# Linear attention with decay feeding a SiLU block: attention by pairs of chunks in 64x64 array tiles

## The chip, the cores and the metric

The kernel runs on one core of a Trainium2 chip. The metric is the device time of one execution in microseconds; the median of three runs is given. Engines are named as in the profile: PE is TensorE (matmul; PEld its weight loads), DVE is VectorE, ACT is ScalarE, POOL is GpSimd, SP is SyncE, which here only issues DMAs.

## What is computed

Two stages, with `q`, `k`, `v` of shape (4, 8, 768, 64) (batch, heads, positions, head dimension) and a decay `lam` per head:

```python
for b in range(nb):                       # blocks of 64 positions
    intra = (qb @ kb.T * Dmask) @ vb      # Dmask[i, j] = lam ** (i - j) for i >= j, else 0
    inter = (qb * lam_pow) @ kv_state     # lam_pow[i] = lam ** (i + 1)
    out[:, :, sl] = intra + inter
    kv_state = lam ** 64 * kv_state + (kb * rev_pow).T @ vb
x = out.transpose(0, 2, 1, 3).reshape(3072, 512)
h = x @ w_in                              # 512 -> 2048
y = (h * sigmoid(h)) @ w_out              # 2048 -> 512
```

All inputs and the output are float32. The kernel works in bf16 on TensorE with float32 sums. The result does not depend on the block length, so a kernel may choose its own chunks.

## The kernel before

**Units.** Attention is worked off in 24 units `u` of U = 128 positions (four batches of six). For each unit, k, q and v come as tiles with a position in each of 128 partitions and (head, dimension) along the row, so that a DMA piece is 64 floats, 256 B. For the first `EARLY` = 8 units all three come as float32 on SP's queue (`raw`, L313), k and q are cast by ACT or DVE into `kq` (L277, L279) and turned by TensorE with an identity (`tr`, L402), then copied to `kqT`. For later units k and q come on POOL's queue, cast on the way (L316), and are turned by a DMA transpose on SP's queue (L416); v still comes by SP. `vd` is v times a power of lam for its position (L284, called from L386).

**Attention of a unit** (heads in `NP` = 4 pairs `m`, a pair filling 128 partitions):
- scores `st_ps` (L427): 8 matmuls of a 64x128 array tile with 128 columns, the two heads of a pair in two row halves; masked by `tri_e` into `st` in two DVE operations
- the new state `d_ps` (L446): 8 matmuls of 128x64 with 64 columns, for all but the last unit of a batch
- from it and the running state `xf`: `y` (L458, add), `xe` (bf16, times lam to the power U) and the next `xf`
- the outputs `x_ps` (L481): 8 matmuls of 128x64 (`st` and `vd`) and, unless the unit is the first of its batch, 8 of 64x64 (`xe` and `kqT`, the term of the state), all summed in one bank
- `xt` (L498): `x_ps` times a power of lam for the query's position, in bf16. This is x, transposed, ready for the first product.

**The two products.** `product1` takes groups of one, two or four units (`groups`): `h_ps` (L518) has 128, 256 or 512 columns per matmul, 512 columns per PSUM bank; ACT applies SiLU (L532) into `g`. `product2` makes a unit's 128 rows of output in `o_ps` (L552), 16 matmuls of 512 columns (of 256, twice, for the first six units and the last), copied by ACT or DVE and stored on ACT's queue.

**Weights.** `w_in` (blocks i0 to i3) and `w_out` (o0 to o3) come on POOL's queue, cast to bf16 on the way. `sequence` (L340) sets the order of loads; POOL reads one element of a landed load (`gated`, L293) before it issues weights, so that the first units' loads get ahead of them.

**Order.** The program is a list of tasks with a key, a cost per engine and the tasks that it depends on. `Planner.order` runs them through a small model of engines, buffers and queues before anything is issued and fixes, once, the order of instructions on every engine. On the chip each engine goes through its list and stops at each instruction until its inputs are there; nothing is reordered. `POOLS` is the number of buffers of each kind; the eight PSUM banks are one pool, `att` allows at most five of them to attention, `one` four to `h_ps` and `two` two to `o_ps`.

Of the kernel before, what the change touches and what calls it, by code (L numbers as in the profile page):

```python
# [8 lines left out]
F32 = mybir.dt.float32  # L9
BF16 = mybir.dt.bfloat16  # L10
# [24 lines left out]
SMALL, CAST, LARGE, HALF, TURN = (256, 16.4, 18.5), (256, 14.0, 31.0), (2048, 92.0, 92.0), (1024, 58.0, 58.0), (1024, 46.0, 46.0)  # L35


class Planner:
# [5 lines left out]
    BEGIN = {"PE": 0.8, "ACT": 6.0, "DVE": 2.7, "POOL": 3.4, "SP": 0.8}  # L44
    FIRST, LAST, AHEAD = {"SP": 1.15, "ACT": 1.15, "POOL": 2.5}, 1.0, 0.75
# [13 lines left out]
    def order(self):  # L59
# [12 lines left out]
        queues = {e: [] for e in ("SP", "POOL", "ACT")}  # L72
        clock = [0.0]
# [49 lines left out]
        while len(out) < len(self.tasks):  # L123
# [9 lines left out]
            for e in free:  # L133
# [34 lines left out]
                free[e] = now + t.on[e]  # L168
                heapq.heappush(events, free[e])
# [20 lines left out]
def kernel(  # L190
# [13 lines left out]
    U = 128  # L204
    NB = S // U
    NU = B * NB
# [4 lines left out]
    EARLY = 8  # L211
# [6 lines left out]
    POOLS = dict(bank=8, raw=9, rv=4, kq=6, kqT=5, vd=4, st=3, xe=3, y=3, xf=3,  # L218
                 xt1=4, xt2=2, xt4=2, g=40, osb=3, osh=4, one=4, two=2, att=5)
# [3 lines left out]
    def tile_of(b, shape, dt, name):  # L223
        if b.tile is None:
            pool = ps if b.pool == "bank" else sb
            b.tile = pool.tile(shape, dt, tag=f"{b.pool}{b.slot}", name=name)
        return b.tile
# [15 lines left out]
    iota_p = const.tile([128, 1], mybir.dt.int32, name="iota_p")  # L243
    nc.gpsimd.iota(iota_p, pattern=[[0, 1]], base=0, channel_multiplier=1)
    row_i = const.tile([128, U], mybir.dt.int32, name="row_i")
    nc.gpsimd.iota(row_i, pattern=[[1, U]], base=-64, channel_multiplier=0)
    tri_e = const.tile([128, U], F32, name="tri_e")
    nc.gpsimd.memset(tri_e, 1.0)
    nc.gpsimd.affine_select(
        out=tri_e, in_=tri_e, compare_op=AL.is_ge, fill=0.0,  # L250
        base=0, pattern=[[1, U]], channel_multiplier=-1,
    )
    pose = const.tile([128, 1], F32, name="pose")
    nc.vector.tensor_scalar(pose, iota_p, -1.0, 64.0, op0=AL.mult, op1=AL.add)
    row = const.tile([128, U], F32, name="row")
    nc.vector.tensor_copy(row, row_i)
# [6 lines left out]
    lam_v = const.tile([128, H], F32, name="lam_v")  # L263
    lam_xe = const.tile([128, NP, U], F32, name="lam_xe")
    lam_be = const.tile([128, NP], F32, name="lam_be")
    nc.scalar.activation(lam_v, log_all, AF.Exp, scale=pose[:, 0:1])
# [20 lines left out]


    gate = const.tile([128, 8], F32, name="gate")
# [17 lines left out]
    def load_unit(key, u):  # L307
        b, blk = divmod(u, NB)
        src = [x[b, :, blk * U:blk * U + U, :].rearrange("h s d -> s h d") for x in (k, q, v)]
        kq, bufs, ts = Buf("kq"), [None] * 3, [None] * 3  # L310

        def plain(e, i):
            nc.sync.dma_start(out=tile_of(bufs[i], [128, H, 64], F32, "raw"), in_=src[i])  # L313

        def casting(e, i):
            nc.gpsimd.dma_start(out=tile_of(kq, [128, 2, H, 64], BF16, "kq")[:, i], in_=src[i])  # L316

        for i in range(3):
            if u < EARLY or i == 2:
                bufs[i] = Buf("raw" if u < EARLY else "rv")  # L320
                ts[i] = add((key, i), {"SP": 0.55}, lambda e, i=i: plain(e, i), bufs=[bufs[i]], nbytes=0.262, kind=SMALL,
                            late=0.3 if u < EARLY else LATE)
            else:
                ts[i] = pool_load((key, i), 0.92, lambda e, i=i: casting(e, i), [kq], 0.262, CAST, LATE)
        raw[u] = kq, bufs, ts
# [3 lines left out]
    def load_w(key, what, j):  # L329
        def go(e):  # L330
            if what == "i":
                cs = slice(512 * j, 512 * j + 512)
                nc.gpsimd.dma_start(out=w_in_bf[:, :, cs], in_=w_in_r[:, :, cs])
            else:
                ks, cs = slice(8 * (j % 2), 8 * (j % 2) + 8), slice(256 * (j // 2), 256 * (j // 2) + 256)
                nc.gpsimd.dma_start(out=w_out_bf[:, ks, cs], in_=w_out_r[:, ks, cs])

        wload[what, j] = [pool_load((key, 0), 0.8, go, [], 1.0486, LARGE if what == "i" else HALF, 1.0)]

    sequence = "u0 i0 i1 u1 i2 u2 i3 u3 u4 u5 u6 o0 o1 u7 o2 o3".split() + [f"u{u}" for u in range(EARLY, NU)]  # L340
    unit, last = None, None
    for n, x in enumerate(sequence):
        j = int(x[1:])
        if x[0] == "u":
            load_unit(n - 100, j)
            unit = j
        else:
            if last != unit and unit < EARLY:
                _, bufs, loads = raw[unit]
                gated((n - 100, -1), loads[0], unit, lambda buf=bufs[0]: buf.tile[:, 0, 0:1])  # L350
                last = unit
            load_w(n - 100, x[0], j)


    groups = [[0], [1], [2], [3], [4, 5], [6, 7], [8, 9], [10, 11]] + [list(range(4 * n, 4 * n + 4)) for n in range(3, NU // 4)]
    group_of = {u: (gi, i) for gi, us in enumerate(groups) for i, u in enumerate(us)}
    xt = [Buf(f"xt{len(us)}") for us in groups]
    xt_done = [[] for _ in groups]
    carry = {}

    chain = {}

    def after(stage, ts):

        ts = ts if isinstance(ts, list) else [ts]
        for t in ts:
            t.deps += chain.get(stage, [])
        chain[stage] = ts

    def Bank():  # L370
        return Buf("bank", Buf("att"))

    def attention(u):
        s = u - 4.0 if u < 4 else u - 5.5
        kq, bufs, (lk, lq, lv) = raw[u]
        kqT, vd, st = Buf("kqT"), Buf("vd"), Buf("st")
        gi, gp = group_of[u]

        def kq_of():
            return tile_of(kq, [128, 2, H, 64], BF16, "kq")  # L380

        def cast(e, i):
            copy(e, kq_of()[:, i], bufs[i].tile)

        def scale_v(e):
            mult(e, tile_of(vd, [128, H, 64], BF16, "vd"), bufs[2].tile,  # L386
                 lam_v[:, :, None].to_broadcast([128, H, 64]))

        if u < EARLY:
            ck = [add((s - 1.0, i), {"DVE": 0.43, "ACT": 0.63}, lambda e, i=i: cast(e, i), deps=[(lk, lq)[i]],  # L390
                      bufs=[bufs[i], kq]) for i in range(2)]
            after("k", ck)
        else:
            ck = [lk, lq]
        cv = add((s - 0.8, 0), {"DVE": 0.7}, scale_v, deps=[lv], bufs=[bufs[2], vd])

        after("v", cv)
        turned = []

        def turn(e, i, m):  # L400
            t = tile_of(banks[i], [128, NP, U], BF16, "tr")
            nc.tensor.transpose(t[:, m, :], kq_of()[:, i, 2 * m:2 * m + 2, :], ident)  # L402

        def t_of():
            return tile_of(kqT, [128, 2, NP, U], BF16, "kqT")

        if u < EARLY:
            banks = Bank(), Bank()
            for i in range(2):
                ts = [add((s - 0.7, i, m), {"PE": 0.056}, lambda e, i=i, m=m: turn(e, i, m), deps=[ck[i]],  # L410
                          bufs=[banks[i], kq]) for m in range(NP)]
                turned.append(add((s - 1.0, 2), {"DVE": 0.65, "ACT": 0.6},
                                  lambda e, i=i: copy(e, t_of()[:, i], banks[i].tile), deps=ts, bufs=[banks[i], kqT]))
        else:
            def dma_turn(e):
                nc.sync.dma_start_transpose(t_of().rearrange("p i m s -> p (i m) s"),  # L416
                                            kq_of().rearrange("p i h d -> p (i h d)"))

            turned.append(add((-150.0, u), {"SP": 1.4}, dma_turn, deps=ck, bufs=[kq, kqT], nbytes=0.393, kind=TURN,
                              late=2.0))  # L420

        st_ps = [Bank() for _ in range(2)]

        def score(e, m):
            for h, r in enumerate(halves):
                t = tile_of(st_ps[h], [128, NP, U], F32, "st_ps")
                nc.tensor.matmul(t[:, m, :], lhsT=t_of()[r, 0, m, :], rhs=t_of()[r, 1, m, :], start=True, stop=True)  # L427

        sc = [add((s - 0.55 + 0.02 * m, 0), {"PE": 0.062}, lambda e, m=m: score(e, m), deps=turned + chain.get("m", []), bufs=st_ps + [kqT])
              for m in range(NP)]  # L430
        mk = [add((s - 0.9, 0), {"DVE": 0.69},
                  lambda e, h=h: mult(e, tile_of(st, [128, 2, NP, U], BF16, "st")[:, h], st_ps[h].tile,
                                      tri_e[:, None, :].to_broadcast([128, NP, U])),
                  deps=sc, bufs=[st_ps[h], st]) for h in range(2)]

        after("s", sc)
        chain["m"] = mk
# [134 lines left out]

    for u in range(NU):
        attention(u)
# [37 lines left out]
```

## Time and profile before

| what | value |
|---|---|
| median of 3 runs | 233.63 us (233.47 to 233.82) |
| the profiled execution | 233.32 us |
| its span, first to last instruction | 231.6 us |
| granted TensorE clock, mean | 0.993 |
| h_ps, L518 | 700 matmuls in the trace, 115.9 us busy |
| o_ps, L552 | 482 matmuls, 105.4 us busy |
| SiLU on ACT, L532 | 96 of 598 ns |
| mask on DVE, st <- st_ps | 48 of 685 ns |
| evacuation xt <- x_ps on DVE | 24 of 688 ns |
| cast loads of k and q on POOL's queue | 32 of 128 KB written |
| transposes on SP's queue | 16 |
| DMA moved | 29.67 MB, 92544 of 102677 packets under 512 B |

Busy times of TensorE overlap, as matmuls are pipelined: what one costs in a stream is the distance from its start to the next start. The page shows the span in 40 slices of 5.8 us, with a digit for the busy share of each engine; a DMA share over 1.00 in the table by stages means that packets of several queues overlap on an engine.

### The profile page before, as it was taken

The page shows a single profiled execution, that of the slowest core. Times are in us where ns is not written, and L with a number is a line of the kernel's source. Part 1 is how long each engine was busy: PE and PEld are TensorE (multiplying, and loading weights), DVE is VectorE, ACT ScalarE, POOL GpSimd, SP SyncE. Part 2 cuts the span into 40 slices and gives each one's busy share as a digit, 9 for nine tenths or more (in the row PEclk, how much of TensorE's full clock was granted, in tenths as well). Part 3 has the DMA queues.
Part 4 walks back from the last instruction along what each step waited for, and adds up shares of the span by engine and source line. Part 5 has one row for each costly group of instructions (what it writes and reads, how often), then busy time and mean ns, then how long its engine had stood idle before and what let it go on. Part 6 is the DMA issues. An engine that isn't in the chain of part 4 may idle for free.

```text
span 231.6 us, 4583 instructions
## 1 busy us (share of the span) xinstructions
PE 212.2 (92%) x1950; PEld 134.5 (58%) x1968; DVE 89.4 (39%) x165; ACT 82.7 (36%) x149; POOL 41.3 (18%) x61
## 2 busy tenths in 40 slices
PE   0547889999999999999999999999999999999994
PEld 0336778878888884686754444444444444444453
DVE  1445285766130007555574663556542111110100
ACT  5431625684433221242521146522323333333221
POOL 3403014922240003350333341011100000000000
PEclk9999979999999999999999999999999999999999
DMA  5999999999999985999999999610101111001112
GB/s 120 203 196 232 217 211 216 167 185 182 159 174 197 152 228 67 195 120 147 167 146 195 193 157 172 123 48 0 48 3 42 48 48 45 14 31 48 73 63 91
DMA packets 102677, 29.67 MB, mean 128 GB/s; under 512 B 92544, under 2 KB 100480, under 8 KB 102656
## 3 DMA queue, kind: packets, MB, share of 16 engines
q0 software_dynamic: 39552, 8.39, 41.3%
q1 hardware_dynamic: 58496, 14.68, 37.8%
q10 hardware_dynamic: 4608, 6.30, 7.9%
q8 instruction: 15, 0.25, 0.4%
q14 instruction: 6, 0.05, 0.1%
HBM read 27.27 MB, written 6.29 MB: 145 GB/s over the span
## 4 chain that ended last, share of the span: by engine, by line
PE 87%; DMA 6%; SPq 2%; DVE 1%; ACT 1%; issue 1%
PE h_ps L518 38%; PE o_ps L552 36%; PE x_ps L481 7%; DMA raw<-in_v_dram 6%; PE d_ps L446 3%; PE st_ps L427 3%; SPq L313 2%; PE tr L402 1%; DVE xt L284 1%; ACT g L532 0%; DVE vd L284 0%; ACT kqT L277 0%; ACT kq L277 0%; DVE xe L284 0%; DVE kqT L279 0%
## 5 line engine op out<-in xcount | busy, mean ns | idle before, releaser
L518 PE MATMUL h_ps<-xt,w_in_bf 128*128 128x128 bf16 (+2 forms) x700 | 115.9, 290 | 1.1 <-DVE xt L284 0.6
L552 PE MATMUL o_ps<-w_out_bf,g 128*128 128x512 bf16 (+1 forms) x482 | 105.4, 330 | 0.7 <-issue 0.5
L532 ACT ACTIVATE g<-h_ps 128x512 bf16<-128x512 f32 x96 | 56.6, 598 | 95.9 <-PE h_ps L518 91.6
L518 PEld LDWEIGHTS <-w_in_bf 128*128 128x128 bf16 x704 | 60.4, 102 | 27.0 <-issue 1.1
L552 PEld LDWEIGHTS <-g 128*128 128x128 bf16 x496 | 47.5, 98 | 32.3
L284 DVE TENSOR_TENSOR st<-st_ps,tri_e 128x512 bf16<-128x512 f32 x48 | 30.9, 685 | 32.1 <-PE st_ps L427 32.1
L279 DVE COPY osb<-o_ps 128x512 f32<-128x512 f32 (+1 forms) x11 | 6.8, 619 | 54.7 <-PE o_ps L552 53.0
L316 POOL DMA_DIRECT2D kq<-in_k_dram x16 | 14.1, 883 | 61.8 <-PE x_ps L481 56.3
L277 ACT ACTIVATE osb<-o_ps 128x256 f32<-128x256 f32 (+1 forms) x20 | 9.6, 479 | 36.0 <-PE o_ps L552 31.0
L284 DVE TENSOR_TENSOR xt<-x_ps,lam_xe 128x512 bf16<-128x512 f32 x24 | 16.5, 688 | 6.3 <-PE x_ps L481 5.9
L402 PE MATMUL tr<-ident,kq 128*128 128x128 bf16 x64 | 7.3, 242 | 11.4 <-POOL gate L293 5.7
L284 DVE TENSOR_TENSOR vd<-raw,lam_v 128x512 bf16<-128x512 f32 x24 | 16.2, 683 | 2.9 <-DMA raw<-in_v_dram 2.9
L316 POOL DMA_DIRECT2D kq<-in_q_dram x16 | 14.2, 890 | 7.3 <-DMA w_out_bf<-in_moe_w_out_dram 6.3
L458 DVE TENSOR_TENSOR y<-d_ps,xf 128x256 f32<-128x256 f32 x16 | 6.8, 425 | 18.5 <-PE d_ps L446 18.5
L277 ACT ACTIVATE kqT<-tr 128x512 bf16<-128x512 bf16 x14 | 8.4, 597 | 11.0 <-PE tr L402 10.9
L284 POOL TENSOR_TENSOR xf<-y,lam_be 128x256 f32<-128x256 f32 x6 | 3.7, 611 | 47.9 <-DVE y L458 47.9
L402 PEld LDWEIGHTS <-kq 128*128 128x128 bf16 x64 | 4.5, 106 | 12.6 <-DVE kq L279 9.3
L427 PE MATMUL st_ps<-kqT 64*128 64x128 bf16 x192 | 10.2, 229 | 1.6 <-ACT kqT L277 0.9
L481 PE MATMUL x_ps<-kqT,xe 64*64 64x128 bf16 x160 | 11.1, 231 | 0.0
L481 PE MATMUL x_ps<-st,vd 128*64 128x128 bf16 x192 | 11.0, 235 | 0.0
L427 PEld LDWEIGHTS <-kqT 64*128 64x128 bf16 x192 | 6.0, 98 | 8.4 <-issue 7.8
L446 PE MATMUL d_ps<-vd,kq 128*64 128x64 bf16 x160 | 9.0, 209 | 1.5 <-DVE vd L284 1.5
(32 smaller groups left out, 55.3 us busy)
## 6 DMA issues: line engine op xcount, KB each, us to landing
raw<-in_v_dram SPq DMA_DIRECT2D x24, 256.0 KB, 6.3
out_dram<-osb ACTq DMA_DIRECT2D x17, 256.0 KB, 2.1
raw<-in_k_dram SPq DMA_DIRECT2D x8, 256.0 KB, 4.9
raw<-in_q_dram SPq DMA_DIRECT2D x8, 256.0 KB, 6.2
w_in_bf<-in_moe_w_in_dram POOLq DMA_DIRECT2D x4, 512.0 KB, 8.0
w_out_bf<-in_moe_w_out_dram POOLq DMA_DIRECT2D x4, 512.0 KB, 13.8
kq<-in_k_dram POOLq DMA_DIRECT2D x16, 128.0 KB, 5.2
kq<-in_q_dram POOLq DMA_DIRECT2D x16, 128.0 KB, 6.5
```

What stands on the lines that cost most here:

```text
L277: nc.scalar.activation(o, i, AF.Copy)
L279: nc.vector.tensor_copy(o, i)
L284: (nc.vector if e == "DVE" else nc.gpsimd).tensor_tensor(o, a, b, op=AL.mult)
L316: nc.gpsimd.dma_start(out=tile_of(kq, [128, 2, H, 64], BF16, "kq")[:, i], in_=src[i])
L402: nc.tensor.transpose(t[:, m, :], kq_of()[:, i, 2 * m:2 * m + 2, :], ident)
L427: nc.tensor.matmul(t[:, m, :], lhsT=t_of()[r, 0, m, :], rhs=t_of()[r, 1, m, :], start=True, stop=True)
L446: nc.tensor.matmul(t[r, m, :], lhsT=kq_of()[:, 0, 2 * m + h, :], rhs=vd.tile[:, 2 * m + h, :], start=True, stop=True)
L458: nc.vector.tensor_tensor(tile_of(src, [128, NP, 64], F32, "y"), d_ps.tile, xf[0].tile, op=AL.add)
L481: nc.tensor.matmul(t[r, m, :], lhsT=lhsT(h, r), rhs=rhs(h, r), start=first, stop=True, skip_group_check=True)
L518: nc.tensor.matmul(t[:, j, :], lhsT=w_in_bf[:, ko, 128 * m:128 * m + 128], rhs=xt[gi].tile[:, ko, :], start=(ko == 0), stop=(ko == KI - 1))
L532: nc.scalar.activation(tile_of(g, [128, per, n], BF16, "g"), bank.tile, AF.Silu)
L552: nc.tensor.matmul(t, lhsT=g.tile[:, j, 128 * gp:128 * gp + 128], rhs=w_out_bf[:, ko, cs], start=(ko == 0), stop=(ko == KO - 1))
```

## The change

Attention goes by 12 pairs of chunks: a pair is 256 positions, a partition holds two neighbouring positions (r = 0, 1) and the partition halves are the two chunks `c` of 128 positions. A row of a load is then two positions, 512 B (later k and q, which are cast on the way, still come in rows of 256 B, one DMA for each r).

- **Tiles.** Scores, outputs and states are all matmuls of 64x64 tiles, with the loops so that four neighbours lie in the four places of the array. The term of the states is a plain 128x128 matmul: `xe` is now a block-diagonal 128x128 matrix for each pair of heads (`xe_all`, zeroed once, then only the two diagonal blocks are written, each by its own DVE operation).
- **Two bursts.** The eight heads go in two halves `g`. After the mask of half i: the states' term and the outputs of half i, the states of the next pair (if i is a pair's second half), the scores of half i+1.
- **PSUM.** `st2` (scores, two banks) and `xd` (outputs and new states, two banks) have one tile each; four single banks stay for `h_ps` (`one`: three), `o_ps` (`two`) and the transposes.
- **Start.** `EARLY` = 5 pairs (ten units) come as float32 and are turned by TensorE; pair 0 comes in two halves of heads (`FINE`). The first group of `product1` has 256 columns and starts on the first two of its four slices when half the heads are done. The first weights wait for v of pair 0's second half (`g0v`), i2 and i3 for k of pair 1, o2 and o3 for k of pair 3.
- **w_out** comes in four blocks of 4x128 whole rows; `product2` uses 512 columns for all but the last unit.
- **Planner.** A switch between tiled and plain matmuls is given 0.095 us.

```diff
-    EARLY = 8
+    EARLY = 5
+    FINE = (0,)
...
-    POOLS = dict(bank=8, raw=9, rv=4, kq=6, kqT=5, vd=4, st=3, xe=3, y=3, xf=3,
-                 xt1=4, xt2=2, xt4=2, g=40, osb=3, osh=4, one=4, two=2, att=5)
+    POOLS = dict(bank=4, st2=1, xd=1, raw=6, rawh=6, rv=3, kq=4, kqT=3, vd=3, st=2, xe=4, y=2, xf=3,
+                 xt2=4, xt4=2, g=40, osb=3, osh=4, one=3, two=2)
...
+    xe_all = const.tile([128, POOLS["xe"], NP, 128], BF16, name="xe_all")
+    nc.vector.memset(xe_all, 0.0)
...
+        def plain(e, i, g, ms):
+            nc.sync.dma_start(out=tile_of(bufs[i, g], [128, 2 * len(ms), 128], F32, "raw"),
+                              in_=src[i][heads(ms)].rearrange("h (p r) d -> p h (r d)", r=2))
+        def casting(e, i, r):
+            nc.gpsimd.dma_start(out=tile_of(kq, [128, 2, 2, H, 64], BF16, "kq")[:, i, r],
+                                in_=src[i].rearrange("h (p r) d -> r p h d", r=2)[r])
...
-    sequence = "u0 i0 i1 u1 i2 u2 i3 u3 u4 u5 u6 o0 o1 u7 o2 o3".split() + [f"u{u}" for u in range(EARLY, NU)]
+    sequence = "u0 g0v i0 i1 u1 g1k i2 i3 u2 u3 o0 o1 g3k o2 o3 u4".split() 
+    sequence += [f"u{n}" for n in range(NU // 2) if f"u{n}" not in sequence]
...
-    groups = [[0], [1], [2], [3], [4, 5], [6, 7], [8, 9], [10, 11]] + [list(range(4 * n, 4 * n + 4)) for n in range(3, NU // 4)]
+    groups = [[0, 1], [2, 3], [4, 5], [6, 7], [8, 9], [10, 11]] + [list(range(4 * n, 4 * n + 4)) for n in range(3, NU // 4)]
...
+        def states(e, ms):
+            t = duo_tile(at)
+            for m in ms:
+                for r in range(2):
+                    for c, p in enumerate(halves[:1] if final else halves):
+                        for h, d in enumerate(halves):
+                            nc.tensor.matmul(t[d, c, 256 + 64 * m:320 + 64 * m], lhsT=kq_of()[p, 0, r, 2 * m + h, :],
+                                             rhs=vd.tile[p, 2 * m + h, r, :], start=first_in(box, c, h), stop=True,
+                                             skip_group_check=True)
...
+                for m in range(2):
+                    for r in range(2):
+                        for c in halves:
+                            for h, d in enumerate(halves):
+                                nc.tensor.matmul(t[c, h, m, r, :], lhsT=t_of()[d, 0, r, 2 * g + m, c],
+                                                 rhs=t_of()[d, 1, :, 2 * g + m, c], start=(m == 0 and r == 0), stop=True,
+                                                 skip_group_check=True)
...
+            def inter(e, i=i, g=g, used=used, box=box_x):
+                t = duo_tile(i)
+                for m in range(2):
+                    for c, x in used:
+                        nc.tensor.matmul(t[:, c, U * m:U * m + U], lhsT=xe_of(x[0])[:, 2 * g + m, :],
+                                         rhs=t_of()[:, 1, :, 2 * g + m, halves[c]],
+                                         start=first_in(box, c, 0) | first_in(box, c, 1), stop=True, skip_group_check=True)
```

## The prediction

> **What bounds the kernel now.** I read the page's busy table and slices first, then the stages, then the chain and single bursts on TensorE.
>
> ```profile
> PE 212.2 (92%) x1950; PEld 134.5 (58%) x1968; DVE 89.4 (39%) x165; ACT 82.7 (36%) x149; POOL 41.3 (18%) x61
> ...
> PE   0547889999999999999999999999999999999994
> ...
> DMA  5999999999999985999999999610101111001112
> ...
> q1 hardware_dynamic: 58496, 14.68, 37.8%
> q10 hardware_dynamic: 4608, 6.30, 7.9%
> ```
>
> From slice 7 on (about 35 us) TensorE is full, although DMA is full too until 75 us. So there are two places to gain: TensorE's work after 32 us, and the holes before it. By stage (us, TensorE busy, loads, DVE, ACT, POOL, clock, DMA):
>
> ```profile
> 0.00:16.70 16.70, 5.07 (x56) 3.34 (x56) 5.33 (x12) 7.49 (x16) 4.36 (x15) 1.00 1.00 172
> 16.70:21.00 4.30, 2.80 (x37) 2.31 (x34) 1.94 (x4) 0.80 (x2) 0.00 (x0) 1.00 1.22 230
> 21.00:32.00 11.00, 9.66 (x136) 8.55 (x136) 5.57 (x13) 5.08 (x9) 2.48 (x4) 0.95 1.19 219
> 32.00:60.00 28.00, 27.43 (x412) 23.35 (x409) 17.21 (x33) 16.43 (x30) 10.71 (x14) 0.96 1.26 187
> 60.00:175.00 115.00, 114.00 (x1051) 71.10 (x1064) 54.53 (x99) 36.58 (x65) 23.74 (x28) 1.00 1.09 135
> ```
>
> Over 98% busy from 32 us, and DVE and ACT under two thirds there: in that part only fewer or denser TensorE instructions shorten the kernel.
>
> One unit of attention (128 positions) costs TensorE two bursts between the big products (start, length, what):
>
> ```profile
> 160.63 0.38 PE L518 MATMUL h_ps<-xt,w_in_bf 128*128 128x512 bf16 x1
> 160.94 0.40 PE L427 MATMUL st_ps<-kqT 64*128 64x128 bf16 x8
> 161.27 0.39 PE L552 MATMUL o_ps<-w_out_bf,g 128*128 128x512 bf16 x1
> ...
> 162.79 0.38 PE L518 MATMUL h_ps<-xt,w_in_bf 128*128 128x512 bf16 x1
> 163.10 0.28 PE L446 MATMUL d_ps<-vd,kq 128*64 128x64 bf16 x6
> 163.32 0.24 PE L481 MATMUL x_ps<-kqT,xe 64*64 64x128 bf16 x2
> 163.49 0.22 PE L446 MATMUL d_ps<-vd,kq 128*64 128x64 bf16 x2
> 163.64 0.35 PE L481 MATMUL x_ps<-kqT,xe 64*64 64x128 bf16 x6
> 163.93 0.41 PE L481 MATMUL x_ps<-st,vd 128*64 128x128 bf16 x8
> 164.27 0.39 PE L552 MATMUL o_ps<-w_out_bf,g 128*128 128x512 bf16 x1
> ```
>
> Big products with 512 columns start 0.216 us apart (162.36, 162.58, 162.79 in the timeline). So the first burst adds 161.27-160.63-0.216 = 0.42 us and the second 164.27-162.79-0.216 = 1.26. The reader should see the price of a change of array shape: st_ps starts 0.31 after the last h_ps instead of 0.216, so 0.095 going in; its last pair starts at 161.12 and the next product at 161.27, 0.15 instead of 0.056, so 0.09 coming out. The second burst changes shape four times inside.
>
> **TensorE, steady part.** Removed: 24 x 0.42 for scores, 16 full second bursts at 1.26, four first units of a batch without the states' term (read the same way at 112.35 us: 0.57) and four last without a new state (174.63: 0.78): 10.2+20.2+2.3+3.1 = 35.8 us.
>
> Added, per pair of chunks (256 positions): 32 score and 32 output matmuls of 64x64 tiles with 128 columns, 32 state matmuls with 64 columns, and 8 plain matmuls for the states' term. In the trace two tiles in different places start 2 to 4 ns apart and the next two 56 ns later (128 columns), or 26 to 32 ns later (64 columns, d_ps). Four tiles at once are not shown, nor 64x64 tiles in four places; two sharing rows (x_ps from vd, d_ps), two sharing columns with different banks (st_ps) and two on the diagonal (xe) are. Bounds: four at a time, 4.5/4 = 1.13 us per pair (64 x 0.056 + 32 x 0.029 = 4.5), and one at a time, 4.5. I take four, since each pairing of places occurs, and the weight loads of d_ps follow each other within some 12 ns on average. Plain: 8 x 0.056 = 0.45, the spacing of h_ps with 128 columns, which these have too. Switches: two bursts, each in and out, 4 x 0.095 = 0.38. Pair: 1.13+0.45+0.38 = 1.96. Twelve make 23.5; the four first pairs of a batch lack half of the plain ones (-0.9), the four last half of the states (-0.5); I add 0.8 for four extra spells in the first pairs, where data come in halves. Sum 22.9, a gain of **12.9 us**.
>
> Transposes on TensorE go from 64 to 80 (five pairs instead of eight units): +0.9. The four 128-column groups of h_ps become 256 wide: by 0.056 against 0.108 per product -0.3 at the most.
>
> **Other engines in that part.** The mask stays at 1.37 us per unit (2 x 0.685), now as one operation of 1024. The state xe is written by two half-partition operations each: 0.43 x 2 more per pair, 10 us on DVE over the kernel, and two more units are cast and copied by DVE and ACT instead of arriving cast (2 x (2 x 0.6 + 2 x 0.6) = 5 us). DVE at 39% and ACT at 36% hide this while each burst has some 8 us to the next (two bursts in 2 x (6.9+1) us); the chain states, y, xe, xf, y, xe of about 3 us must fit there too. Without that cover it would be 15 us. SP issues 25 loads and 7 transposes instead of 40 and 16, POOL 28 casts instead of 32: lighter queues, priced at nothing, as TensorE waited for neither after 32 us. The whole-row stores of the first six units (6 instead of 12 on ACT) and w_out by rows of 1024 B instead of 512 end in the backlog of h_ps work and are priced at nothing too. The memset of xe_all stands on DVE ahead of pose and row; four times a bf16 512-column result at 0.69 bounds it at 2.8 us, so done by 3.6, and ACT's first Ln waits for lam until 4.01: hidden (else vd, at 7.69, moves by as much).
>
> **Waits added.** Scores and outputs have one PSUM tile each. Scores already wait for the mask before; outputs now wait also for the evacuation before (0.69) and for y reading the states in the same tile (two of 0.43), some 2 us against 8 between bursts. The second outputs of a pair wait for the next pair's transpose and vd: behind them on TensorE stand all big products in its order, so a late transpose would stop TensorE by as much as it is late. Its loads are issued two or three pairs (16 us each) ahead and a transpose lands in 5.3 us for half the size: nothing.
>
> **The start.** On full speed the work done by 32 us is 96 h_ps x 0.056, 36 transposes x 0.056 and three and a half units of attention (4.8): 12.2 us, so 19.8 us are lost there. What decides is when loads land. First, rows of 512 B. q1 (nearly all 256-B packets): 37.8% of 16 x 231.6 us over 58496 packets is 23.9 ns each; q10 (mean 1367 B) 63.5 ns. The straight line gives 33 ns for 512 B against 2 x 23.9, so 0.69 of the time. Bounds: no gain, and half. The casts of k and q, and vd, of unit 0 begin as their loads land, at 5.20, 6.41, 7.69: 1.2 us per 256 KB, which becomes 0.85.
>
> Second, a moved gate: POOL's first weights wait for the first unit's k now (gate at 5.23, issue 5.61) and would wait for v of the second half of pair 0, the sixth piece: 5.2 + 5 x 0.85 = 9.5. Behind the gate on POOL stand all weights. The four w_in blocks land now 6.7, 9.1, 10.2 and 6.9 us after issue (12.3, 15.7, 19.1, 29.0). From 9.9 on the first lands at 16.6, the others 3.7 apart (20, 24, 28), as the second gate, k of pair 1, has passed by then (pair 1 streams from 8 to 13 us while POOL waits). So the first h_ps comes at 16.6, as now (16.76). But then two pairs are ready instead of one unit: each block feeds 2 x 16 x 0.108 = 3.5 us of h_ps. Work: 13.8 h_ps, 4 attention, 1.8 transposes; until about 20 us it runs at half speed (h_ps 16.76: 16 in 1.89 us). I get its end at 34 to 35 us, so 15 us lost: a gain of **5.0 us**. Ends: 0 (plan and arrivals disagree, as for v at 19.4 now, where TensorE stood 1.5 us), and 9 (19.6 us of work done by 31). I take the middle for the order of each engine's work is fixed and slips are likely.
>
> [...]
>
> **Sum.** Span 231.6 - 12.9 + 0.9 - 0.3 - 5.0 = 214.3. The profiled execution took 233.32, 1.7 more than its span; the median is 233.63, 0.3 more again. Forecast **216.3 us**, by itself 211 to 220.
>
> **Rivals.**
> A, the start gains nothing, or bursts don't merge (outputs and scores apart: 2 more spells a pair, 12 x 0.38 = 4.6): 221. For it: the gate is 4.3 us later and plans slip. Against: two pairs feed each block. Chance 0.17.
>
> B, only two tiles at a time: per pair 2.25+0.83 = 3.08, 13.4 us more: 230. For it: four were never seen. Chance 0.08.
>
> C, slower, by PSUM: eight banks shared become four for h_ps, o_ps and transposes, since scores and outputs hold two each for good. With three h_ps banks of 0.86 us each ACT must return one in 2.6 us; silu is 0.6, but casts and copies of pairs are 1024 wide (2 x 0.63) and stand ahead of it in ACT's queue. It decides the sign from 17 us, 0.18 for each of 96 banks; at 0.2 each, 19 us: 235. Against: ACT waited 91.6 us for h_ps, TensorE none for ACT there. Chance 0.06.
>
> D, slower: column tiles load weights one after another, so that no two tiles overlap: 96 x 0.029 to 0.056, 4.5+0.83 = 5.33 per pair, 40 us more than forecast: 257. Break-even is at 1.75 tiles at a time. d_ps starts six 64-column loads within 60 ns, which speaks against: 0.03. [...]
>
> **How the numbers follow.** Forecast 0.66, A 0.17, B 0.08, C 0.06, D 0.03. The range 210 to 225 holds forecast and A. About 0.2% can be told from no change; near zero falls next to nothing: faster 0.90, same 0.01, slower 0.09.
>
> **What would show it.** Spells of tiled matmuls two per pair, each about 0.9 to 1.1 us between big products; four tiles starting within 15 ns; the first h_ps near 16.6 with few gaps after; TensorE busy over 98% from 35 us. Wrong if TensorE waits for ACT g or xt in the middle, if tiles come 28 ns apart, or if the first w_in lands after 18.

## The result, and the profile after

The changed kernel takes 274.5 us (273.19 to 278.7, 4 runs) against 233.55 for the kernel before: a ratio of 1.1746 (95% interval 1.1672 to 1.182). Some runs show a lower granted clock and take longer; the ratios leave them out, here the one of 278.7 us. Forecast were 216.3 us, with 210 to 225 as the range. The profiled execution took 273.79 us, with a span of 271.9.

The page of the changed kernel: busy times, and the slices of TensorE, of its granted clock and of DMA (40 slices of 6.8 us).

```profile
PE 210.8 (78%) x2198; PEld 125.8 (46%) x2224; DVE 100.9 (37%) x162; ACT 83.1 (31%) x138; POOL 33.7 (12%) x51
...
PE   1669999989970069839199999999999999999400
...
PEclk9999999999995559977869999999999999999955
DMA  5999999999945999999998383011001111111110
```

TensorE has no more to do than before (210.8 us busy against 212.2); the 40 us are holes, around slice 13, around slices 18 and 20, and at the end, and stretches at half clock. The stages of the changed kernel (columns as before: stage, length, then TensorE, its loads, DVE, ACT, POOL, clock, DMA, GB/s):

```profile
21.00:32.00 11.00, 11.00 (x134) 8.98 (x133) 5.75 (x11) 6.63 (x10) 0.00 (x0) 1.00 1.19 216
...
78.00:98.00 20.00, 2.25 (x57) 1.55 (x55) 0.69 (x1) 0.00 (x0) 1.75 (x2) 0.60 1.09 77
98.00:127.00 29.00, 22.42 (x236) 13.23 (x233) 13.60 (x20) 4.56 (x8) 7.00 (x8) 0.80 1.97 127
127.00:260.00 133.00, 120.68 (x1041) 63.02 (x1052) 41.34 (x64) 38.05 (x65) 3.51 (x4) 0.97 0.39 52
260.00:272.00 12.00, 0.00 (x0) 0.00 (x0) 0.00 (x0) 0.00 (x0) 0.00 (x0) 0.50 0.11 42
```

The start is as full as was hoped: from 21 to 32 us TensorE is busy throughout. Then it stands still from 79 to 97, runs on at half clock for a while (0.80 granted from 98 to 127), and in the last 12 us no engine computes at all, while DMA still moves 42 GB/s. Two more stretches without work on TensorE, from 114.3 to 120.1 and from 129.7 to 135.4 us, are in its list of waits without a releaser ("issue" means that the profile shows none; in total, times, longest, us):

```profile
PE h_ps L621 <- issue: 6.7, 6, 5.7
PE o_ps L655 <- issue: 6.3, 4, 5.8
```

TensorE's and SP's instructions at the first hole, in the timeline (start, length, what):

```profile
79.44 0.41 PE L487 MATMUL xd<-vd,kq 64*64 64x64 bf16 x16
97.55 0.64 PE L548 MATMUL st_ps<-kqT 64*64 64x128 bf16 x16 [17.70 <-DMA kqT<-kq]
```

```profile
66.67 29.99 SPq L458 DMA_TRANSPOSE kqT<-kq  x2
```

Scores of pair 5 wait 17.7 us for the DMA transpose of its k and q, and SP needs 30 us to issue two transposes. The slices of DMA between 70 and 95 us (0.625 us each; first the mean busy share of the 16 DMA engines, then GB/s):

```profile
DMA  9999849992911111111111111999999999999999
GB/s 322 319 298 205 118 79 186 124 55 49 43 41 43 42 43 43 40 43 40 42 43 43 42 42 40 63 75 69 71 74 71 72 72 72 68 65 85 112 114 112
```

From 76.9 to 85.6 us a tenth to a fifth of the DMA engines' time is used and 40 to 43 GB/s flow: about two sixteenths of the 322 in the first of these slices (40, an estimate). The trace does not say on which engine a packet runs, but it has every packet's time. I counted how many packets of 2048 B of the store queue overlap. After, e3 and e7 spend 78, 79 and 63% of the time with any such packet at the number given; in before, e1 and e2 the number rises and falls with each store, and the table gives what it rises to (for short times 17 or 18):

| kernel | first dimension of a store in memory | packets of 2048 B that overlap |
|---|---|---|
| before | 128 rows | 16 |
| after | r = 2 | 2 |
| e1 | 64 rows, two DMAs | 15 to 16 |
| e2 | 128 rows | 16 |
| e3 (before with r first) | r = 2 | 2 |
| e7 (before with r first) | r = 4 | 4 |

The line of the change behind it is in `product2`; it is not among the lines shown with the change. As partition r * 64 + a of the output tile holds row 2 * a + r of a block of 128, the store has to put the rows back in order:

```diff
-                nc.scalar.dma_start(out=out[128 * u:128 * u + 128, cs], in_=osb.tile)
+                nc.scalar.dma_start(out=out[128 * u:128 * u + 128, cs].rearrange("(a r) f -> r a f", r=2), in_=osb.tile)
```

It moves the same bytes in the same packets (2048 B, 84 ns each), but with r = 2 in front two run at a time. By the packets' time that is an estimated 64 x 84 ns = 5.4 us for 256 KB, where 16 at a time take 0.7. Summed over the run, packets of 2048 B are under way for 150 us after and for 27 us in e2, with 23 whole stores in each. The other DMAs go at the pace of the stores meanwhile: from 78 to 84 us the trace has 94 packets of 2048 B (stores), 93 of 512 B (loads) and 92 of 128 B (casts). It looks as if each queue had its next piece waiting on the same two engines; that is an inference, as no run shows the engine of a packet.

### The profile page after: what moved, and what is told of

Same layout as the page of the kernel before. It is cut to its first block, busy times and chain, and to the rows that moved or that the text cites. A ratio compares the mean times of both kernels' runs of the same rounds, so it can differ in the third digit from the quotient of the medians.

```text
span 271.9 us, 4974 instructions
## 1 busy us (share of the span) xinstructions
PE 210.8 (78%) x2198; PEld 125.8 (46%) x2224; DVE 100.9 (37%) x162; ACT 83.1 (31%) x138; POOL 33.7 (12%) x51
## 4 chain that ended last, share of the span: by engine, by line
PE 69%; DMA 13%; issue 6%; DVE 4%; ACT 1%; ACTq 1%; SPq 0%; DVEq 0%
PE h_ps L621 31%; PE o_ps L655 29%; DMA kqT<-kq 11%; PE xd L585 3%; PE st_ps L548 3%; DMA raw<-in_v_dram 2%; PE xd L575 2%; PE xd L487 2%; DVE vd L296 1%; DVE xt L296 1%; DVE st L296 1%; PE tr L443 1%; ACTq L671 1%; DVE xe_all L296 1%; ACT osb L289 1%
## 5 line engine op out<-in xcount | busy, mean ns | idle before, releaser
L621 PE MATMUL h_ps<-xt,w_in_bf 128*128 128x256 bf16 (+1 forms) x567 | 135.9, 322 | 7.1 <-issue 6.7
L655 PE MATMUL o_ps<-w_out_bf,g 128*128 128x512 bf16 (+1 forms) x383 | 125.2, 377 | 6.9 <-issue 6.3
L296 DVE TENSOR_TENSOR st<-st_ps,tri 128x1024 bf16<-128x1024 f32 x24 | 29.2, 1219 | 25.9 <-PE st_ps L548 25.9
L296 DVE TENSOR_TENSOR xt<-xd,lam_xe 128x512 bf16<-128x512 f32 x24 | 16.6, 690 | 47.5 <-PE xd L585 29.4
L291 DVE COPY osb<-o_ps 128x512 f32<-128x512 f32 x13 | 9.0, 692 | 55.7 <-PE o_ps L655 50.6
L548 PE MATMUL st_ps<-kqT 64*64 64x128 bf16 x384 | 11.4, 242 | 19.2 <-DMA kqT<-kq 17.7
L548 PEld LDWEIGHTS <-kqT 64*64 64x64 bf16 x384 | 7.6, 119 | 23.2 <-DMA kqT<-kq 17.8
L296 DVE TENSOR_TENSOR vd<-raw,lam_v 128x1024 bf16<-128x1024 f32 (+1 forms) x13 | 14.7, 1136 | 1.5 <-DMA raw<-in_v_dram 1.5
L296 DVE TENSOR_TENSOR xe_all<-y,lam_be 64x256 bf16<-64x256 f32 (+1 forms) x34 | 13.7, 403 | 0.7
L585 PE MATMUL xd<-st,vd 64*64 64x128 bf16 x384 | 10.7, 233 | 1.5 <-DVE st L296 1.5
L289 ACT ACTIVATE kqT<-tr 128x1024 bf16<-128x1024 bf16 (+1 forms) x11 | 9.4, 866 | 7.0 <-PE tr L443 5.5
L289 ACT ACTIVATE osb<-o_ps 128x512 f32<-128x512 f32 (+1 forms) x12 | 6.7, 560 | 12.6 <-PE o_ps L655 12.6
```

Of the source, the lines that this page charges most:

```text
L289: nc.scalar.activation(o, i, AF.Copy)
L291: nc.vector.tensor_copy(o, i)
L296: (nc.vector if e == "DVE" else nc.gpsimd).tensor_tensor(o, a, b, op=AL.mult)
L548: nc.tensor.matmul(t[c, h, m, r, :], lhsT=t_of()[d, 0, r, 2 * g + m, c], rhs=t_of()[d, 1, :, 2 * g + m, c], start=(m == 0 and r == 0), sto ...
L585: nc.tensor.matmul(t[d, c, U * m:U * m + U], lhsT=vd.tile[p, 2 * (2 * g + m) + h, r, :], rhs=st.tile[p, 2 * h + m, U * r:U * r + U], start ...
L621: nc.tensor.matmul(t[:, j, :], lhsT=w_in_bf[:, ko, 128 * m:128 * m + 128], rhs=xt[gi].tile[:, ko, :], start=(ko == 0), stop=(ko == KI - 1))
```

## The experiments

Two theories were set against each other. S: the stores hold two DMA engines, and everything that needs all 16 waits there. P: the pairs starve by themselves, since k and q of the later pairs come in twice as large units through POOL's queue with few buffers.

**e1, each store as two DMAs.**

```diff
-                nc.scalar.dma_start(out=out[...].rearrange("(a r) f -> r a f", r=2), in_=osb.tile)
+                rows = out[128 * u:128 * u + 128, cs].rearrange("(a r) f -> r a f", r=2)
+                for r in range(2):
+                    nc.scalar.dma_start(out=rows[r], in_=osb.tile[halves[r]])
```

> The changed kernel with each store of 128 rows as two DMAs, one for each r (64 partitions to every second row); the order of all other work is the same. Theory S (a store whose first dimension in memory is r = 2 runs on two of the 16 DMA engines; in the trace of after, the 2048-byte packets of the store queue overlap two at a time, in before 16): the transposes land in time, the 30 us wait at 66 and the 15 us tail go, 214 to 224 us. Theory P (pairs starve: k and q come in pairs through POOL's queue in 256-byte pieces, with four and three buffers, whatever the stores do): the wait at 66 stays, only the tail shrinks, 255 to 265 us.

231.21 us, ratio 0.9897 to the kernel before (0.9795 to 0.9999). 43 us are gone by this alone: P falls as the main cause. It is still above the 214 to 224 of S, as a part of the wait for the transposes stays (4.5 us).

**e2, x in the natural order, so that a store is 128 neighbouring rows again.**

```diff
-                mult(e, t[...].rearrange("p m (c s) -> p c m s", c=2), duo_tile(i)[:, :, 0:256]..., lam_xe[...])
-                nc.scalar.dma_start(out=out[...].rearrange("(a r) f -> r a f", r=2), in_=osb.tile)
+                for c in range(2):
+                    at = 256 * (gp // 2) + 128 * c
+                    mult(e, t[:, 2 * g:2 * g + 2, at:at + 128].rearrange("p m (a r) -> p m r a", r=2),
+                         duo_tile(i)[:, c, 0:256].rearrange("p (m r a) -> p m r a", m=2, r=2),
+                         lam_xe[:, 2 * g:2 * g + 2, :].rearrange("p m (r a) -> p m r a", r=2))
+                nc.scalar.dma_start(out=out[128 * u:128 * u + 128, cs], in_=osb.tile)
```

> The changed kernel with x evacuated in the natural order of positions (two DVE operations of 256 per half instead of one of 512, written with a stride of two), so that a store is one DMA of 128 partitions to 128 whole neighbouring rows. Theory S: as e1, within 3 us, 214 to 225; DVE gets 24 x 0.2 = 5 us more work, hidden. Theory P: 255 to 265.

227.69 us, ratio 0.9799 (0.9725 to 0.9872), a little above S's interval too: with good stores the change is about 2% faster than the kernel before. The longest wait of TensorE in e2 after the start is the same one, much shorter (in total, times, longest, us):

```profile
PE st_ps L548 <- DMA kqT<-kq: 3.3, 1, 3.3
```

Of the 45.7 us between the spans of after and e2, 14.4 are this wait (17.7 against 3.3), 11.5 the two stretches without a releaser, which e2 doesn't have, and 13.6 the end, from the last copy of output to the end of the span (16.6 against 3.0). The rest, some 6 us, I have not split; stretches at half clock are in it. What TensorE waited for in the two stretches is not shown. It was not ACT, which is idle in both (0.00 us busy). In the first, a fetch of 16 KB on the queue named instruction takes 4.0 us, where others take 0.9 to 1.9; that is a lead and no more.

**e3 and e7, the kernel before with that store alone.** In e3 the line above goes into the kernel before with r = 2, in e7 with r = 4.

```diff
-                nc.scalar.dma_start(out=out[128 * u:128 * u + 128, cs], in_=osb.tile)
+                nc.scalar.dma_start(out=out[128 * u:128 * u + 128, cs].rearrange("(a r) f -> r a f", r=2), in_=osb.tile)
```

> The kernel before with the store's access pattern of the change, r first, and nothing else; the rows within each block of 128 of its output are in another order. Theory S: each whole store holds two engines for 64 x 84 ns = 5.4 us, 24 of them 129 us out of the 165 us in which outputs come; the loads of units 8 and up, which need all 16 engines, wait behind, and the last store ends later: 243 to 275 us. Theory P: the stores were not it, 233 to 238.

> The kernel before with the rows of each store cut by four instead of two ((a r) f as r a f with r = 4) and nothing else; rows of the output within each block of 128 are in another order. Theory S with the engines given by the first dimension: four engines of 16, 2.7 us per store, 65 us of 165 on each: between before and e3, 236 to 255, and the 2048-byte packets overlap four at a time. If any such pattern is slow (by its addresses): as e3, 285 to 292. If r = 2 alone is bad: 233 to 235.

e3 takes 287.23 us, against 233.29 for the kernel before, and e7 254.91, ratio 1.0934 (1.0807 to 1.1061). So the line alone costs the old kernel 54 us, more than S had allowed, and with r = 4 22. It isn't that r = 2 is special, nor that every such pattern is equally slow: the time follows the number of packets that run at a time, 2, 4 or 16, while one packet takes 84 to 86 ns in all three. That fits S; that the shared thing is an engine is S's reading and not shown. TensorE in the slices of e3 (of a run of 293.2 us) and of e7, one under the other, with holes where transposes are late (TensorE waits 23.2 us for them in e3, 10.8 in e7) and an empty end:

```profile
PE   1568899999948738987099680999999999999700
```

```profile
PE   0458789999999989829999957999999999999980
```

**e4, e1 with neighbouring matmuls in one place of the array.** Only the loops over places (c, h) and over what goes through them (m, r) are exchanged, in scores, outputs and states.

```diff
-                    for r in range(2):
-                        for c in halves:
-                            for h, d in enumerate(halves):
+                for c in halves:
+                    for h, d in enumerate(halves):
+                        for m in range(2):
+                            for r in range(2):
```

> e1 with the loops of scores, outputs and states turned round, so that eight neighbouring matmuls lie in the same 64x64 place of the array instead of four in four places. The same instructions, the same sums. If four tiles at a time are what makes the bursts short (the forecast): 64 x 0.056 + 32 x 0.029 = 4.5 us per pair instead of 1.13, 40 us more than e1, 255 to 262. If the gain came from fewer switches alone: within 5 us of e1.

231.67 us, e1's time (231.21): the 40 us were wrong. The edit puts eight neighbours in one place in the states alone; in scores and outputs it is four. Bursts of e2 and, below, of e4, whose TensorE instructions differ here only by that order:

```profile
134.41 0.42 PE L585 MATMUL xd<-st,vd 64*64 64x128 bf16 x16
134.66 0.42 PE L487 MATMUL xd<-vd,kq 64*64 64x64 bf16 x32
134.91 0.40 PE L548 MATMUL st_ps<-kqT 64*64 64x128 bf16 x16
```

```profile
137.41 0.45 PE L585 MATMUL xd<-st,vd 64*64 64x128 bf16 x16
137.66 0.78 PE L487 MATMUL xd<-vd,kq 64*64 64x64 bf16 x29
```

Sixteen outputs, four in a row in each place, are as fast as before (0.25 us to the next group in both). 32 states, eight in a row in each place, go from 0.25 to some 0.6 us. The starts show how: the sixteen outputs start 13 to 14 ns apart in e4, while in after the next one in the same place starts 56 ns later. So the four places do work at once, but neighbours in the program need not lie in different places: a run of four in one place costs nothing in these bursts, a run of eight does. In the total it can't be seen. e4's time agrees with the second expectation, "fewer switches alone", and yet the starts show that this is not the reason.

**e5, e2 with pieces of 256 B.**

```diff
-                              in_=src[i][heads(ms)].rearrange("h (p r) d -> p h (r d)", r=2))
+                              in_=src[i][heads(ms)].rearrange("h (p r) d -> p r h d", r=2))
```

> e2 with the float32 loads of k, q and v in pieces of 256 B again (one for each position), all else the same. If rows of 512 B brought what the prediction said (0.69 of the time), each pair of 1.57 MB takes 7.2 us instead of 5.1: the first pair lands 2 us later, DMA stays full some 9 us longer, the first transposes come later still, and the wait of 5 us at 78 grows: 6 to 12 us over e2, 233 to 240. If rows don't matter: within 2 us of e2.

242.12 us, ratio 1.0383 (1.0323 to 1.0443), 14.4 us over e2. Rows of 512 B are worth more than expected here, and not at the place that was expected: the wait for the transposes fell to 0.9 us, but loads that miss the order's plan stop TensorE at the start:

```profile
32.85 0.64 PE L487 MATMUL xd<-vd,kq 64*64 64x64 bf16 x32 [14.21 <-DVE xt L296]
33.42 0.82 PE L623 MATMUL h_ps<-xt,w_in_bf 128*128 128x256 bf16 x3
```

VectorE waits 13.37 us for v of pair 1, which it can use at 30.9 us, and the first h_ps comes at 33.4 us. Part of these 14 us may be the order, which was planned for the faster loads, and not the rows themselves; no run separates the two.

**e6, six early pairs; e9, a gate ahead of the late casts.** Both start from e2, to remove what is left of the wait for pair 5.

```diff
-    EARLY = 5
+    EARLY = 6
...
-    kq=4, kqT=3
+    kq=6, kqT=4
```

> e2 with six pairs instead of five as float32 and turned by TensorE (EARLY = 6), with six kq and four kqT buffers so that the order can be planned. Pair 5 then needs no cast load and no DMA transpose. If the wait at 78 (3.3 us of TensorE for kqT, and half clock after it, some 8 us together) is what is left of the gap to the forecast: 219 to 223, with 0.9 us more of transposes on TensorE. If the wait only moves to pair 6: 226 to 230.

```diff
-    sequence = "u0 g0v i0 i1 u1 g1k i2 i3 u2 u3 o0 o1 g3k o2 o3 u4".split()
+    sequence = "u0 g0v i0 i1 u1 g1k i2 i3 u2 u3 o0 o1 g3k o2 o3 u4 g4v".split()
```

> e2 with one more gate on POOL: the cast loads of k and q for pair 5 and up wait for v of pair 4 to land. In e2 they begin at 39 us and share DMA with pairs 3 and 4. If that sharing delays what TensorE needs first: 222 to 226, a little faster. If pair 5 is late anyway, its casts now begin only near 55 and the wait at 78 grows by some us: 228 to 240.

e6 takes 231.69 us (ratio 0.9931, 0.9897 to 0.9965), 4 us over e2 and above both ranges: the wait moved on and grew (4.8 us in two waits, 1.5 more than in e2). e9 takes 223.99 us, ratio 0.9601 (0.9536 to 0.9666), and the wait is gone altogether. But the transposes don't come earlier. SP's first two in e2 and, below, in e9:

```profile
65.75 16.82 SPq L458 DMA_TRANSPOSE kqT<-kq  x2
```

```profile
66.44 15.62 SPq L458 DMA_TRANSPOSE kqT<-kq  x2
```

They end at 82.6 and 82.1 us. What moved is TensorE's fixed order: in e2 it is through with its work ahead of the scores of pair 5 at 78.9 us and waits until 82.1, in e9 more of the big products stand ahead of them and it comes to them at 85.4. Presumably the plan, which reckons with the gate, expected the transposes later and so nearer to when they come; that is not shown. The expectation had the right range (222 to 226) for another reason, less sharing with pairs 3 and 4.

**e10 and e11, the start.** Both from e9: an earlier first gate, and pair 0 in one piece.

```diff
-    "u0 g0v i0 ..."
+    "u0 g0k i0 ..."     # e10
...
-    FINE = (0,)
+    FINE = ()           # e11
```

> e9 with POOL's first gate on k of pair 0's second half (the fourth piece) instead of v (the sixth): w_in's first block is issued and lands 1.5 to 2 us earlier. The prediction held that this landing sets the first h_ps. If so the first h_ps comes at 18.3 to 18.8 instead of 20.3 and the time falls by 1 to 2 us, to 222 to 223. If VectorE sets it (it is busy without a gap from 12 to 24 us in e9, and the second half's mask and xt stand in its queue): the first h_ps stays at 20 or later, as the pieces of pair 0 and 1 lose DMA time to the weights: 224 to 227.

> e9 with pair 0 in one piece like the others (FINE empty): three loads of 512 KB, operations of 1024 in place of two of 512, the first gate on v of the whole pair. If VectorE's work sets the start: 14 operations become half as many longer ones, some 2 us of fixed cost less, but the first mask begins 3 us later; the first h_ps at 20 to 22, 223 to 226. If the landing of the first pieces set it, it moves by 2.5 us: 226 to 228.

e10 takes 226.35 us (ratio 0.973, 0.9684 to 0.9777) and e11 223.21 (0.9571, 0.9526 to 0.9617). The first products in e9, e10 and e11:

```profile
20.32 1.46 PE L623 MATMUL h_ps<-xt,w_in_bf 128*128 128x256 bf16 x6
```

```profile
19.09 2.55 PE L623 MATMUL h_ps<-xt,w_in_bf 128*128 128x256 bf16 x11
```

```profile
18.48 0.39 PE L623 MATMUL h_ps<-xt,w_in_bf 128*128 128x256 bf16 x2 [0.53 <-DMA w_in_bf<-in_moe_w_in_dram]
```

In e10 the first block of weights lands at 17.1 us instead of 19.5, and the first h_ps comes 1.2 us earlier, between the two expectations. The landing doesn't set it: the last wait of TensorE ahead of it is 1.72 us for VectorE's mask. The order changed with the gate too; in e10 the scores and states of pair 1 stand behind the first h_ps and no longer ahead of it. What was gained is lost again: from 21 to 32 us TensorE in e10 is busy for 8.61 of 11 us instead of 11.00, and what it waits for there is VectorE (vd, y and xt), not a DMA. So the time came out as in the second expectation, but the reason given there, DMA time lost to the weights, is not seen. In e11, with pair 0 whole, VectorE is through with pair 0's xt at 17.9 us instead of 19.7. The first h_ps comes 1.8 us earlier than in e9, earlier than either expectation had it, and waits 0.53 us for the weights themselves; the time is e9's within 1 us. e11 is the fastest of all kernels here, but not clearly faster than e9.

## Why the prediction was wrong

**The step that failed** is the one on the stores: "The whole-row stores of the first six units (6 instead of 12 on ACT) and w_out by rows of 1024 B instead of 512 end in the backlog of h_ps work and are priced at nothing too." It counted the stores and not their shape. The change turned all of them, and by their new first dimension each runs two packets at a time for an estimated 5.4 us instead of 0.7. Replacing that store (e2) is worth 274.5 - 227.7 = 46.8 us, and putting it into the old kernel costs 54. No rival had it; C and D, the two on the slower side, named PSUM banks and weight loads, and neither shows: TensorE's lists of waits in after and e2 name no wait for SiLU, ACT is idle in the two stretches without a releaser (0.00 us busy), and tiles overlap (four start 3 to 4 ns apart). The chance of 0.09 given to "slower" stood on these two alone, so that it came true is luck.

**"Nothing" for the added wait** on the transposes failed with it: "so a late transpose would stop TensorE by as much as it is late". It did, by 17.7 us, and the half clock after the hole (0.50 until 102.5 us) added to that. Even with good stores 3.3 us of it stayed (e2), until e9's order came to the scores later (3.7 us off the time). The prediction had the mechanism and put its price at nothing, from how early the loads are issued; the two transposes take 30 us there, and 17 with good stores, and it had gone by 5.3 us for one "for half the size".

**TensorE's bursts**, read one by one, were right in size. A full second burst in the changed kernel, between products of 108.44 and 109.81 us:

```profile
108.44 0.38 PE L655 MATMUL o_ps<-w_out_bf,g 128*128 128x512 bf16 x1
108.66 0.39 PE L575 MATMUL xd<-kqT,xe_all 128*128 128x128 bf16 x4
108.97 0.42 PE L585 MATMUL xd<-st,vd 64*64 64x128 bf16 x16
109.22 0.42 PE L487 MATMUL xd<-vd,kq 64*64 64x64 bf16 x32
109.47 0.40 PE L548 MATMUL st_ps<-kqT 64*64 64x128 bf16 x16
109.81 0.61 PE L621 MATMUL h_ps<-xt,w_in_bf 128*128 128x256 bf16 x2
```

It adds 109.81 - 108.66 = 1.15 us. The first kind, read in e9 from 90.25 to 91.14, adds 0.89: together 2.04 per pair against 1.96 priced, and tiles start four at a time 3 to 4 ns apart, every 56 ns (128 columns) or 32 ns (64). Rival B falls. What was missed is how often bursts come apart: after 32 us I count 35 spells of attention in e9, where two for each of the ten pairs still due make 20; at 0.19 us a spell that is some 2.9 us. In the sum the bursts therefore gained less than priced. An estimate from the trace adds up all spells after 32 us, each from its first start to that of the next product, with the ordinary spacing taken off, and 0.216 us wherever the trace lacks a product's record: some 31 us before, as the prediction's prices give too, and some 23 in e9, where its prices give 18.4 for the same matmuls. So about 8 us were gained there and not 12.6. This is the half of rival A that came true.

**The start.** Gate at 9.29 (9.5 said), issue at 9.84 (9.9), landing at 17.0 (16.6) were right in the changed kernel, but "the first h_ps comes at 16.6" was not: it comes at 19.8, behind these lines of it.

```profile
17.48 0.64 PE L585 MATMUL xd<-st,vd 64*64 64x128 bf16 x16 [1.53 <-DVE st L296]
...
19.21 0.65 PE L487 MATMUL xd<-vd,kq 64*64 64x64 bf16 x32 [0.66 <-DVE xt L296]
19.79 1.46 PE L621 MATMUL h_ps<-xt,w_in_bf 128*128 128x256 bf16 x6
```

VectorE, to whose work the prediction gave no time of its own in the start, is the engine that it waits for: masks, vd and states of pair 0 stand in its queue. That is 3.2 us, and 3.7 in e9. e9's 224.0 is 7.7 us from the forecast; the start (3.7) and the bursts (4.8) account for it, as estimates that together come out 0.8 too high. Two smaller terms were off as well. A load's packet of 512 B takes 27 ns in after and one of 256 B 18 in before (medians), so 0.75 of the time for the same bytes and not 0.69; and the wider first groups save 256 x 0.056 - 128 x 0.108 = 0.5 us by the prediction's own prices, not 0.3 at the most. The gain by bursts is there, at some 8 us, and 512-B rows are worth their place (e5); no run separates what the start gained. With another store the change is 2% faster (e2), with e9's gate as well 4%, not 7.4.

## What to carry to other kernels

When a layout change reorders rows, write down the access pattern of every DMA that it touches, the stores too, and look at the first dimension on both sides: with 2 and 4 in front of a store 2 and 4 packets ran at a time here instead of 16, which cost the kernel before 54 and 22 us. The sign of it in the profile was a DMA share of 0.1 to 0.2 with a constant 40 to 43 GB/s, while TensorE waited 17.7 us for a transpose; count how many packets of one queue overlap. Two fixes brought the 274.5 us down: splitting the DMA along that dimension (e1, 231.2), and moving the reordering into an operation that copies the data anyway (e2, 227.7).

## What the hardware showed that I had not expected

- While stores ran two packets at a time, the other transfers hardly moved: from 76 to 86 us casts and transposes were under way, and the rate was 40 to 43 GB/s in all, after 322 at 70 us. 23 stores that by themselves take an estimated 5 us longer cost the kernel nearly 50 us.
- Matmuls of 64x64 tiles are started four at a time even when four in a row go to the same place of the array (e4); with eight in a row 32 states take 0.6 us instead of 0.25.
- During the hole of 18 us the granted clock fell to half (0.50 from 82.1 us), and it stayed there for the first 4.5 us of work after it (until 102.5 us); it was at half again from 120.1 to 126.4, after the second hole. So a hole costs more than its length here.
